# Other start addresses for the operands of the large matrix products

## The chip, the cores and the metric

The kernel runs on one core of a Trainium2 chip. The metric is the device time of one execution in microseconds (us); the time given is the median of several executions. The core has five engines with a queue each: TensorE (PE in the profile; its weight loads are listed apart as PEld), VectorE (DVE), ScalarE (ACT), GpSimd (POOL) and SyncE (SP), which here issues the DMAs. TensorE multiplies a stationary operand (up to 128 x 128, loaded by a weight load) with a moving operand (128 partitions, up to 512 columns), both read from the on-chip memory SBUF, and adds into PSUM. SBUF has 128 partitions; an address below is a byte offset within a partition, the same in all of them.

## The reference

A recurrent attention, then two mixing blocks, all in float32 (cut to what is computed):

```python
for t in range(S):                       # B=2, H=8, S=768, D=48
    cur = einsum('bhd,bhe->bhde', u * kt, vt)
    y[:, :, t] = einsum('bhd,bhde->bhe', rt, state + cur)
    state = wt[..., None] * state + einsum('bhd,bhe->bhde', kt, vt)
x = y as (B, S, 384)
h = gelu(x @ w_in)                       # 384 -> 1024, halves u and v
v_s = einsum('ts,bsd->btd', w_sg, norm(v) * g_ln) + b_sg
x = x + (u * v_s) @ w_out                # 512 -> 384
h = relu(xT @ w_tok1) @ w_tok2           # along the tokens, 768 -> 256 -> 768
u = x + hT
out = u + relu(u @ w_ch1) @ w_ch2        # 384 -> 1536 -> 384
```

## The kernel before, in words

The 1536 tokens (two batches of 768) are cut into 12 chunks of 128. Every product that isn't small is done three times: an operand is split into a high part, rounded to a 4-byte format that TensorE takes at one column per cycle (float32r in the listing), and a low part, the rest. `prod` (lines 254 to 259) issues high x high, high x low and low x high into one PSUM tile, so lines 257, 258 and 259 hold 588 matmuls each, 1764 in all. 1440 of them have 384 moving columns, 216 have 256 (`Hu`) and 108 have 512 (`Hv`); the stationary operand is always 128 x 128, and each matmul brings its own weight load.

The order is written out by hand. `ORDER` interleaves the attention of all chunks (letters for scores, states, outputs) with the input product `Hv` and `Hu`, the gate product `Gk` and the output product `Op`; `LAST` goes on with the rest of these, the token products `T1p` and `T2p` and the first quarter of the channel product `C1`; `rest` (line 483) then alternates one tile of `C1` for a quarter of the tokens with the three matmul groups of `C2` that use the quarter before. Each engine runs its instructions in that order. Weights arrive as pairs of 32-bit words in staging tiles `st`, are put together by ScalarE and VectorE (lines 214 to 219) and split into high and low (lines 224 to 226). SyncE issues all DMAs.

What matters here is where tiles lie. A pool reserves its buffers one after the other from the left end of SBUF, or from the right end with `side="right"`, when it is opened; a tile of a pool takes one of its buffers. The order of the pools and their sizes thus set every address before the program runs. The pools are: `dcst` (the identity matrix and small constants), `small` (statistics), `a2` (23 buffers of 2048 bytes: normalized gate operands `vh`, `vl`, token hidden `hh`, `hl`, channel hidden high `ch`), `a15` (36 of 1536: `x1h`, `uh`, `ul`, `gh`, `gl`, `cl` and others), `pw` and `psg` (six weights of 6144 each), `pst` (staging), later `pw2a` (`c10`, `c11`) on the left and `pxt` (the transposed input `xt`) on the right, where `pw2b` (`c12`) takes its place in the end. Since 2048, 1536, 6144 and 3072 are multiples of 512, all buffers of a pool have the same residue modulo 512, and slices of operands start at multiples of 512 bytes. `PAD` (line 37) gives three filler tiles, in 4-byte words, that nothing reads or writes.

Of the kernel before, what the change touches and what calls it, by code (L numbers as in the profile page):

```python
# [7 lines left out]
F32 = mybir.dt.float32  # L8
# [11 lines left out]
P = 128  # L20
# [13 lines left out]
ADDED = 7  # L34


PAD = 88, 32, 24


HALF = (slice(0, 64), slice(64, P))  # L40
# [33 lines left out]
class Dense:  # L74


    def __init__(self, tc, ctx, ins, out):
        self.tc, self.nc, self.ins, self.out = tc, tc.nc, ins, out
        self.ctx = ctx
        pool = lambda n, bufs, **kw: ctx.enter_context(  # L80
            tc.tile_pool(name=n, bufs=bufs, reuse_waits="tile", **kw))
        self.cst = pool("dcst", 1)
        self.cst.tile([P, PAD[0]], F32, name="pad0")
        self.ident = self.cst.tile([P, P], F32, name="ident")
        self.small = pool("small", 3, side="right")
        self.small.tile([P, PAD[2]], F32, name="pad2", bufs=1)
        self.pa2 = pool("a2", 23)
        self.pa15 = pool("a15", 36)
        self.pw = pool("pw", 6)
        self.psg = pool("psg", 6)  # L90
        self.pst = pool("pst", 4)
        self.ps3 = pool("mm3", 3, space=PSUM)
        self.banks = [self.ps3]
        self.x, self.v, self.vh, self.vl, self.uT = {}, {}, {}, {}, {}
        self.w, self.xt, self.xc, self.mv = {}, {}, {}, {}
        self.sums = None
        self.x1, self.u, self.gT, self.hid = {}, {}, {}, {}
        self.gps, self.gt, self.ops, self.tps, self.tok, self.ups = ({} for _ in range(6))
        self.todo, self.loaded, self.pipe = [], [], []

        self.free = [(self.pst, "st", 99)] * 4 + [(self.pw, "w", 2)] * 2
        self.n = 0
# [40 lines left out]
    def consts(self):  # L143
        nc = self.nc
        make_identity(nc, self.ident)
        self.g = self.cst.tile([P, FF // P], F32, name=self.nm("g"))
        self.mhalf = self.cst.tile([P, 1], F32, name=self.nm("mhalf"))
        nc.gpsimd.memset(self.mhalf, -0.5)
        warm = self.cst.tile([P, 1], F32, name=self.nm("warm"))
        nc.scalar.activation(warm, self.mhalf, AF.Gelu_apprx_tanh)  # L150
        self.cst.tile([P, PAD[1]], F32, name="pad1")

# [758 lines left out]
```

## Time and profile before

| | us |
|---|---|
| median of three runs | 390.88 (390.84 to 391.51) |
| the profiled execution | 391.98 |
| its span, first to last instruction | 390.3 |
| TensorE busy | 379.9 (97%) |
| VectorE busy | 233.5 (60%) |
| ScalarE busy | 187.8 (48%) |
| GpSimd busy | 133.1 (34%) |
| chain that ended last, TensorE's share | 83% |

The profiled execution is one of its own, so sums made from its rows are compared with its own 391.98 us first. In a timeline each row begins with the start and the length of an instruction in us; the length of a matmul includes the time its last column needs to come out, while the next one is already running, so the rate is read from start to start and not from the length. The chain follows the last instruction back to what released it, step by step.

### The profile page before, as it was taken

The page shows a single profiled execution, that of the slowest core. Times are in us where ns is not written, and L with a number is a line of the kernel's source. Part 1 is how long each engine was busy: PE and PEld are TensorE (multiplying, and loading weights), DVE is VectorE, ACT ScalarE, POOL GpSimd, SP SyncE. Part 2 cuts the span into 40 slices and gives each one's busy share as a digit, 9 for nine tenths or more (in the row PEclk, how much of TensorE's full clock was granted, in tenths as well). Part 3 has the DMA queues.
Part 4 walks back from the last instruction along what each step waited for, and adds up shares of the span by engine and source line. Part 5 has one row for each costly group of instructions (what it writes and reads, how often), then busy time and mean ns, then how long its engine had stood idle before and what let it go on. Part 6 is the DMA issues. An engine that isn't in the chain of part 4 may idle for free.

```text
span 390.3 us, 7950 instructions
## 1 busy us (share of the span) xinstructions
PE 379.9 (97%) x3229; PEld 354.8 (91%) x3229; DVE 233.5 (60%) x396; ACT 187.8 (48%) x427; POOL 133.1 (34%) x149
## 2 busy tenths in 40 slices
PE   8899999999999999999999999999999999999994
PEld 3487788889999799999999999999999999999993
DVE  7999998889797575794486674782133114211320
ACT  3699878887345795754546674741111111111000
POOL 2325577763543356567544651350000000000000
PEclk9999999999999999999999999999999999999998
DMA  7575375453361014322433242400010001000110
GB/s 238 172 215 181 100 246 155 122 156 114 94 214 42 2 40 123 107 66 71 123 102 102 81 126 78 121 3 0 3 44 18 1 0 62 0 2 0 64 40 27
DMA packets 15581, 33.68 MB, mean 86 GB/s; under 512 B 2352, under 2 KB 5680, under 8 KB 15536
## 3 DMA queue, kind: packets, MB, share of 16 engines
q1 hardware_dynamic: 15536, 33.09, 27.9%
q8 instruction: 27, 0.44, 0.5%
q14 instruction: 18, 0.15, 0.1%
HBM read 30.72 MB, written 2.36 MB: 85 GB/s over the span
## 4 chain that ended last, share of the span: by engine, by line
PE 83%; POOL 4%; ACT 3%; issue 3%; DVE 3%; DMA 2%; SPq 1%; POOLq 0%; ACTq 0%
PE mm L257 23%; PE mm L258 23%; PE mm L259 23%; PE py L623 3%; PE pa L582 2%; PE py L608 2%; DMA st<-in_dram 1%; PE tr L282 1%; POOL vs L367 1%; PE pkv L641 1%; DMA kr<-in_dram 1%; PE mm L567 1%; PE mm L420 1%; PE py L617 1%; PE pt L595 1%
## 5 line engine op out<-in xcount | busy, mean ns | idle before, releaser
L399 DVE SCALAR_TENSOR_TENSOR cl<-mm,ch 128x384 fp32r<-128x384 f32 x48 | 26.5, 556 | 83.9 <-ACT ch L398 83.9
L398 ACT ACTIVATE ch<-mm 128x384 fp32r<-128x384 f32 x48 | 23.4, 492 | 93.1 <-PE mm L259 93.0
L217 DVE SCALAR_TENSOR_TENSOR st<-st 128x384 int32<-128x384 int32 (+1 forms) x50 | 30.3, 607 | 9.5 <-ACT st L215 7.9
L219 DVE SCALAR_TENSOR_TENSOR st<-st 128x384 int32<-128x384 int32 (+1 forms) x50 | 33.2, 665 | 1.7
L214 ACT ACTIVATE st<-st 128x384 f32<-128x384 f32 (+1 forms) x50 | 25.8, 517 | 9.3 <-DMA st<-in_dram 9.3
L588 POOL TENSOR_SCALAR_AFFINE_SELECT A<-A 128x512 f32<-128x512 f32 x24 | 18.3, 770 | 33.5 <-ACT A L587 32.0
L215 ACT ACTIVATE st<-st 128x384 int32<-128x384 uint32 (+1 forms) x50 | 25.5, 510 | 0.0
L369 ACT ACTIVATE gh<-vs 128x384 fp32r<-128x384 f32 x16 | 8.4, 524 | 32.9 <-POOL vs L367 32.9
L367 POOL TENSOR_TENSOR vs<-vs,uT 128x384 f32<-128x384 f32 x16 | 19.2, 1205 | 11.6 <-DVE vs L365 11.6
L560 POOL TENSOR_TENSOR rk<-kr 112x512 f32<-112x512 f32 x12 | 19.0, 1580 | 11.4 <-DMA kr<-in_dram 11.4
L257 PE MATMUL mm<-xt,wuh 128*128 128x256 f32 x72 | 20.8, 289 | 0.0
L259 PE MATMUL mm<-xt,wul 128*128 128x256 f32 x72 | 20.3, 282 | 0.0
L258 PE MATMUL mm<-xt,wuh 128*128 128x256 f32 x72 | 20.3, 282 | 0.0
L534 DVE TENSOR_TENSOR_SCAN wf<-wf,scan 112x516 f32<-112x516 f32 x12 | 19.0, 1583 | 1.6 <-DMA wf<-in_dram 1.6
L548 DVE TENSOR_TENSOR_SCAN wf<-wf,scan 112x516 f32<-112x516 f32 x12 | 17.8, 1480 | 0.4
L391 POOL TENSOR_TENSOR x1l<-x,x1h 128x384 fp32r<-128x384 f32 x12 | 14.0, 1173 | 10.4 <-ACT x1h L390 10.4
L125 PE MATMUL mm<-scan 112*128 112x512 bf16 x49 | 14.2, 431 | 3.1 <-DVE scan L673 1.7
L556 DVE TENSOR_TENSOR kr<-kr,wf 112x1024 f32<-112x1024 f32 x12 | 15.9, 1328 | 1.2 <-DVE wf L548 0.2
L257 PE MATMUL mm<-ch,c20h 128*128 128x384 f32 x48 | 16.1, 336 | 0.2 <-DVE o L454 0.2
L257 PE MATMUL mm<-woh,gh 128*128 128x384 f32 x48 | 16.2, 338 | 0.0
L259 PE MATMUL mm<-woh,gl 128*128 128x384 f32 x48 | 16.1, 336 | 0.0
L257 PE MATMUL mm<-uh,c10h 128*128 128x384 f32 x48 | 16.1, 336 | 0.0
(188 smaller groups left out, 1233.3 us busy)
## 6 DMA issues: line engine op xcount, KB each, us to landing
st<-in_dram SPq DMA_DIRECT2D x38, 384.0 KB, 3.4
kr<-in_dram SPq DMA_DIRECT2D x12, 448.0 KB, 4.3
st<-in_dram SPq DMA_DIRECT2D x18, 256.0 KB, 4.2
wf<-in_dram SPq DMA_DIRECT2D x12, 227.5 KB, 2.9
vn<-in_dram SPq DMA_DIRECT2D x12, 192.0 KB, 4.5
out_dram<-o SPq DMA_DIRECT2D x12, 192.0 KB, 1.9
bsg<-in_dram SPq DMA_DIRECT2D x2, 192.0 KB, 3.9
ub<-in_dram SPq DMA_DIRECT2D x1, 3.5 KB, 4.6
```

The lines of the kernel that those rows point to most:

```text
L214: nc.scalar.activation(high.bitcast(F32), high.bitcast(F32), AF.Copy, scale=REBIAS)
L215: nc.scalar.activation(low, low.bitcast(U32), AF.Copy, scale=TOP3, bias=FLOOR)
L217: nc.vector.scalar_tensor_tensor(low, high, -2 ** 31, low, op0=ALU.bitwise_and, op1=ALU.bitwise_or)
L219: nc.vector.scalar_tensor_tensor(low, high, 3, low, op0=ALU.logical_shift_left, op1=ALU.bitwise_or)
L257: mm(out, w[0], x[0], start=first, stop=False, skip_group_check=True)
L258: mm(out, w[0], x[1], start=False, stop=False, skip_group_check=True)
L259: mm(out, w[1], x[0], start=False, stop=last, skip_group_check=True)
L367: nc.gpsimd.tensor_tensor(t, t, self.uT[d, h], op=ALU.mult)
L398: nc.scalar.activation(hi, ps, AF.Relu)
L399: nc.vector.scalar_tensor_tensor(lo, ps, 0.0, hi.bitcast(F32), op0=ALU.max, op1=ALU.subtract)
L534: nc.vector.tensor_tensor_scan(WF[i][:, WCOL + 2:], WF[i][:, :NHP * CW], scan1.rearrange("p h c -> p (h c)"), 0.0, op0=ALU.mult, op1=ALU.add)
L560: nc.gpsimd.tensor_tensor(RK[i][:PR], KR[i][:, 0], KR[i][:, 1], op=ALU.mult)
```

## The change

The pools are opened in another order, and the fillers are other ones. `dcst` moves from the left end to between `a15` and `pw`; `small` moves from the right end to the left, after `pst`; fillers may now stand in four places (a size of 0 opens none), and two of them are used, of 24 words (96 bytes) each.

```diff
-PAD = 88, 32, 24
+PAD = 24, 0, 0, 24
...
-        self.cst = pool("dcst", 1)
-        self.cst.tile([P, PAD[0]], F32, name="pad0")
-        self.ident = self.cst.tile([P, P], F32, name="ident")
-        self.small = pool("small", 3, side="right")
-        self.small.tile([P, PAD[2]], F32, name="pad2", bufs=1)
+        if PAD[0]:
+            pool("pada", 1).tile([P, PAD[0]], F32, name="pad0")
         self.pa2 = pool("a2", 23)
         self.pa15 = pool("a15", 36)
+        self.cst = pool("dcst", 1)
+        self.ident = self.cst.tile([P, P], F32, name="ident")
+        if PAD[1]:
+            pool("padb", 1).tile([P, PAD[1]], F32, name="pad1")
         self.pw = pool("pw", 6)
         self.psg = pool("psg", 6)
         self.pst = pool("pst", 4)
+        self.small = pool("small", 3)
+        if PAD[2]:
+            pool("padc", 1).tile([P, PAD[2]], F32, name="pad2")
+        if PAD[3]:
+            pool("padd", 1, side="right").tile([P, PAD[3]], F32, name="pad3")
...
-        self.cst.tile([P, PAD[1]], F32, name="pad1")
```

The start residues modulo 512, in bytes, as the two built programs have them:

| pool | before | after |
|---|---|---|
| `a2`, `a15`, identity | 0 | 256 |
| `pw`, `psg`, `pst` | 0 | 128 |
| `pw2a` (`c10`, `c11`) | 0 | 0 |
| `pxt` (`xt`), `pw2b` (`c12`) | 0 | 384 |

And the distance of the moving from the stationary operand, modulo 512, for the 1764 matmuls of lines 257 to 259:

| product | matmuls, columns | before | after |
|---|---|---|---|
| `Hv`, `Hu` (`xt` and `wv`, `wu`) | 108 of 512, 216 of 256 | 0 | 256 |
| `Gk` (`vh`, `vl` and `sg`) | 288 of 384 | 0 | 384 |
| `Op` (`gh`, `gl` and `wo`) | 144 of 384 | 0 | 384 |
| `T1p` (`x1h`, `x1l` and `t1`) | 72 of 384 | 0 | 128 |
| `T2p` (`hh`, `hl` and `t2`) | 72 of 384 | 0 | 384 |
| `C1` with `c10`, `c11` | 288 of 384 | 0 | 256 |
| `C1` with `c12` | 144 of 384 | 0 | 384 |
| `C2` (`ch`, `cl` and `c2`) | 432 of 384 | 0 | 128 |

The instructions of the executed path, their order on each engine, their shapes and what they wait for stay as they are.

## Rows read from the trace of the kernel before

**Rows 1.** The page: TensorE and the others, granted clock, the chain by engine.
```profile
PE 379.9 (97%) x3229; PEld 354.8 (91%) x3229; DVE 233.5 (60%) x396; ACT 187.8 (48%) x427; POOL 133.1 (34%) x149
...
PEclk9999999999999999999999999999999999999998
...
PE 83%; POOL 4%; ACT 3%; issue 3%; DVE 3%; DMA 2%; SPq 1%; POOLq 0%; ACTq 0%
```

**Rows 2.** Busy us per stretch: PE, PEld, DVE, ACT, POOL, then clock, DMA.
```profile
50.00:100.00 50.00, 50.00 (x645) 44.69 (x644) 45.57 (x70) 39.18 (x87) 32.65 (x34) 1.00 0.52 155
...
300.00:350.00 50.00, 50.00 (x291) 50.00 (x290) 11.71 (x22) 7.88 (x16) 0.00 (x0) 1.00 0.04 13
```

**Rows 3.** Timeline of TensorE, 299.9 to 302.9 us: start, length, instruction.
```profile
299.90 0.33 PE L257 MATMUL mm<-uh,c10h 128*128 128x384 f32 x1
...
300.42 0.33 PE L257 MATMUL mm<-uh,c11h 128*128 128x384 f32 x1
...
302.85 0.33 PE L259 MATMUL mm<-ch,c20l 128*128 128x384 f32 x1
```

**Rows 4.** Timeline of the weight loads in the same stretch.
```profile
300.42 0.19 PEld L258 LDWEIGHTS mm<-ul,c11h 128*128 128x128 f32 x1
```

**Rows 5.** Timeline of TensorE, two runs of 512 columns (ends of each).
```profile
44.11 0.39 PE L259 MATMUL mm<-wvh,xt 128*128 128x512 f32 x1
...
45.47 0.39 PE L259 MATMUL mm<-wvh,xt 128*128 128x512 f32 x1
...
134.33 0.40 PE L258 MATMUL mm<-wvl,xt 128*128 128x512 f32 x1
...
136.19 0.28 PE L257 MATMUL mm<-xt,wuh 128*128 128x256 f32 x1
```

**Rows 6.** Timeline of TensorE, a run of 256 columns (its ends).
```profile
150.05 0.28 PE L257 MATMUL mm<-xt,wuh 128*128 128x256 f32 x1
...
151.25 0.28 PE L258 MATMUL mm<-xt,wuh 128*128 128x256 f32 x1
```

**Rows 7.** Timeline of TensorE, warm-up in bf16, merged rows of two windows.
```profile
6.13 2.97 PE L125 MATMUL mm<-scan 112*128 112x512 bf16 x13
...
8.51 0.59 PE L125 MATMUL mm<-scan 112*128 112x512 bf16 x2
```

**Rows 8.** Timeline of TensorE, second token product near 246 us.
```profile
245.87 0.27 PE L420 MATMUL mm<-ident,x 128*128 128x128 f32 x1
...
246.16 0.34 PE L258 MATMUL mm<-t2l,hh 128*128 128x384 f32 x1
...
246.88 0.34 PE L259 MATMUL mm<-t2h,hl 128*128 128x384 f32 x1
```

**Rows 9.** Timeline of TensorE, three transposes, merged.
```profile
203.55 0.49 PE L420 MATMUL mm<-ident,x 128*128 128x128 f32 x3
```

**Rows 10.** Line 257 by stretch: matmuls, weight loads, clock, DMA.
```profile
45.90:130.70 84.80, 33.43 (x101) 19.08 (x101) 1.00 0.46 141
...
134.00:171.30 37.30, 24.78 (x76) 14.37 (x77) 1.00 0.29 85
171.30:201.70 30.40, 19.13 (x57) 10.66 (x57) 1.00 0.28 79
201.70:364.00 162.30, 102.46 (x304) 57.08 (x304) 1.00 0.14 42
...
365.70:391.00 25.30, 12.11 (x36) 6.76 (x36) 0.95 0.14 50
```

**Rows 11.** The chain that ended last, in order of time: start, length, what.
```profile
130.71 0.57 DVE x L632
...
180.03 0.81 POOL x1l L391
...
200.63 1.04 POOL t2l L226
...
384.77 0.56 DVE o L454
```

## Prediction

> **What bounds the kernel now.** The page comes first, [rows 1]: TensorE is busy 97% of the span, the clock line reads 9 in all slices but the last, and the chain that ended last is 83% TensorE. A busy TensorE isn't a TensorE at its peak, so the next view is the busy time by stretch, [rows 2]: from 50 to 100 us VectorE is busy for 45.57 of 50 us, close behind TensorE; from 300 to 350 us VectorE has 11.71 of 50 and TensorE all 50. The second half is therefore TensorE's alone; the first has two engines near the limit. The granted clock is 1.00 in these stretches, the upper of the two levels, 2.4 GHz.
>
> The third view is the order in time within a quiet stretch, [rows 3]. From 299.90 to 302.85 us there are 17 matmuls of 384 columns, one after the other: 2.95 / 17 = 173.5 ns from start to start. 384 columns at 2.4 GHz are 160.0 ns. So 13.5 ns of each matmul, 8% of it, is not columns, and no wait is named for it. Beside each matmul runs the weight load of the next one; it starts with the matmul [rows 3, 4], so the moving operand and the next stationary operand are read at the same time, from the first column on.
>
> Then I ask on what the 13.5 ns depends. With 512 columns a run of six takes 45.47 - 44.11 = 1.36 us, 226.7 ns each, against 213.3 of columns: 13.4 ns [rows 5]. With 256 columns ten take 151.25 - 150.05 = 1.20 us, 120.0 each, against 106.7: 13.3 ns [rows 6]. The excess is a fixed time, that of 32 columns (13.3 ns). A 128-column weight tile of 4-byte words is 512 bytes in a partition, and 32 columns are 128 bytes of it. The bf16 matmuls of the warm-up, which move half the bytes per column, don't have it: 13 in a row take 2.97 us and the last 2 of them 0.59, so 11 spacings take 2.38 us, 216.4 ns, 3.1 over the columns [rows 7]. They too read both operands from one place (the same tile), so a common address alone is no harm at half the byte rate.
>
> Is the excess a constant price? The trace says no. Another run with 512 columns takes 136.19 - 134.33 = 1.86 us for 8, 232.5 ns each, with the same shapes, lines and address residues as the run at 226.7 [rows 5]. And after the transposes of the second token product four 384-column matmuls take 246.88 - 246.16 = 0.72 us, 180 ns each [rows 8]. What differs there is only how the two read streams stand to each other in time after an interruption. A price that moves with that looks like two streams that get in each other's way, and an address shift is another way to move them apart.
>
> **The change part by part.** It adds, removes and reorders no executed instruction: pads and pool order set addresses alone. That part costs nothing, and there is no new wait and no transfer that is issued at another place. Vector, scalar and GpSimd instructions and the DMAs get other addresses too; the trace shows no price by address for them, their nearest evidence is that their operands also start at residue 0 now, and I put them at 0 with a bound of 0.5 us either way (about what a run of this kernel varies by: 390.84 to 391.51).
>
> What is left is the excess of the 1764 products with 4-byte operands. My reading: the weight load and the moving operand start at the same residue, the moving stream has to let the load go ahead by 128 bytes, and that is the 32 columns. When they start 128, 256 or 384 bytes apart and advance alike, they never meet, and the excess falls to what bf16 shows. To be careful with rounding I take 2.7 ns for that (between 2.38/11 = 216.4 and 216.0, less 213.3). The gain is then 13.5 - 2.7 = 10.8 ns per matmul. Bounds: 0 if the excess isn't an address matter, and at most 13.5 (no excess left). Downwards, the price of streams that don't fall into step, 180 - 173.5 = 6.5 ns lost per matmul.
>
> Could the weight load become the limit instead? Three transposes with a 128-column weight load each take 0.49 us, one alone 0.27, so two spacings take 0.22: 110 ns per load [rows 8, 9]. The products aim at 162.7, 109.4 and 216 ns; only those of 256 columns touch that limit, and they lose nothing that I count.
>
> How many of the 1764 lie where TensorE sets the pace? By the windows of line 257 [rows 10], times three (lines 258 and 259 have the same counts within one):
> 45.9 to 130.7 us: 101 x 3 = 303, 3.3 us. VectorE is 91% busy there [rows 2] and will be what is late next; I count half, 1.6.
> 134 to 171.3: 76 x 3 = 228, 2.5 us, counted in full.
> 171.3 to 201.7: 57 x 3 = 171, 1.8 us. The chain runs through GpSimd here [rows 11], from 180.03 to the low half of a weight at 200.63; how much of that GpSimd chain itself hangs on TensorE the chain doesn't settle. Half, 0.9.
> 201.7 to 364: 304 x 3 = 912, 9.8 us, in full: ScalarE and VectorE only follow there.
> 365.7 to 391: 36 x 3 = 108, 1.2 us, in full.
> Before 45.9 us and between 130.7 and 134 the chain is on other engines (from 130.71 VectorE's addition and what follows it, [rows 11]); nothing is counted. The end after 384.77 us (last addition, store) stays.
> Sum: 1.6 + 2.5 + 0.9 + 9.8 + 1.2 = 16.0 us. The profiled execution took 391.98 us, its span 390.3 and 1.7 around it; it would be 376.0. It was 1.1 over the median of 390.88, so the median becomes 374.9: 375. If all 1764 counted, 1764 x 10.8 ns = 19.1 us, 372. With half the gain per matmul the sum is 8.0 us, 383.
>
> The Trainium skill, "TensorE: Matmul & The Clock Gate", section "Back-to-back issue gap", gives N/2.4 + 2.5 ns for an isolated gap, 162.5 at 384 columns, which the trace contradicts by 11 ns in each matmul of rows 3; by that figure the sum would be 16.3 us (an estimate from the page). The same skill speaks against the change: "SBUF — State Buffer", section "Who interferes with whom", holds that TensorE's two read ports are independent and that "PE and ACT never wait on anyone", so addresses could not matter and the time would stay. The trace neither shows nor excludes that for two streams of one engine; the unequal runs of rows 5 lean against it.
>
> **The rivals.**
> No change, 390.9. The 32 columns could be a fixed step of loading 4-byte weights, whatever the address. For: the same 13.3 to 13.5 ns at three widths, undisturbed by the other engines [rows 2, 3, 5, 6], and at distance 0 alone the trace can't show a dependence on distance. Against: 232.5 and 180 ns [rows 5, 8]. The change then does only what it says, and the addresses do nothing. Chance 0.20.
>
> Part of the excess, 384. If only some of the distances are free (the products lie at 128, 256 and 384, and the load that runs beside a product's last matmul belongs to the next), or the load merely crosses the moving stream later, a third to two thirds goes: 5 to 11 us. Chance 0.18.
>
> Slower, 400. At distance 0 the streams fall into a steady step: 173.5 ns holds for hundreds of matmuls, and disturbed runs come back to it. That may be the best they can do: the load first, the moving stream one block behind, no further meeting. With unequal starts the step may never form, and each matmul pays what the disturbed ones do. The place is every 384-column product, 1440 of them; the price 180 - 173.5 = 6.5 ns, 9.4 us in all, and nothing hides it since TensorE is the bound: 400. It decides as soon as the mean spacing in the channel stage is above 173.5. For: the disturbed runs of rows 5 and 8 are slower than the steady ones. Against: they are disturbed by interruptions, with the same residues. Chance 0.20.
>
> **How the numbers follow.** Full removal 0.42 at 375 (own range 371 to 381), part of it 0.18 at 384, nothing 0.20 at 390.9, slower 0.20 at 400. Faster is 0.60. What can be told from no change is about 0.2%, 0.8 us: same 0.20, slower 0.20. Cases of both signs hold the chance, so the range is wide: below 372 I leave 0.05, and above 396, where the upper half of the slower case lies, about 0.12.
>
> **What would show it.** Right: from 300 us on the spacing of 384-column matmuls at 162 to 164 ns, about 110 with 256 columns and 216 with 512; TensorE waiting more in 46 to 131 us on VectorE and ScalarE, and near 200 us on GpSimd; the channel stage from 202 us to the end about 11 us shorter. Wrong: 173.5 again (the fixed price); three different spacings by pool (C1 from the first late pool at 256, its last third at 384, C2 at 128), which is the partial case and says which distance is good; or 175 and more (the slower case).

## The result and the profile after

The changed kernel is slower: 393.62 us (392.84 to 394.80, six executions) against 390.99 us (390.83 to 392.40, six) in the same comparison, ratio 1.0062 with a 95% interval of 1.0047 to 1.0078. The medians differ by 2.63 us, the interval means 1.8 to 3.0 us lost, where 16 us of gain had been forecast. The profiled execution took 392.84 us.

The page of the kernel after, busy time, granted clock and chain by engine (to be held against [rows 1]; all line numbers are 5 higher than before):

```profile
PE 382.2 (98%) x3229; PEld 357.6 (91%) x3229; DVE 232.7 (59%) x396; ACT 188.1 (48%) x427; POOL 132.6 (34%) x149
...
PEclk9999999999999999999999999999999999999998
...
PE 93%; ACT 4%; DVE 1%; issue 0%; ACTq 0%
```

The same 3229 matmuls at the same granted clock keep TensorE busy 2.3 us longer, while the other engines move by less than 1 us. TensorE's share of the chain rose from 83% to 93%, so nothing else became the bound; the products themselves got slower.

Where, the order in time shows. Timeline of TensorE after, the channel stage (start, length, instruction), one round of 18 products, to be held against [rows 3]:

```profile
299.84 0.33 PE L262 MATMUL mm<-uh,c10h 128*128 128x384 f32 x1
...
301.41 0.34 PE L262 MATMUL mm<-ch,c20h 128*128 128x384 f32 x1
...
302.99 0.33 PE L262 MATMUL mm<-uh,c10h 128*128 128x384 f32 x1
```

The first nine, `C1` (six with `c10` and `c11` at 256, three with `c12` at 384), take 301.41 - 299.84 = 1.57 us, 174.4 ns each; the nine of `C2`, whose operands are 128 bytes apart, take 1.58 us, 175.6 each; the round 3.15 us, 175.0 on average, where [rows 3] gave 173.5. Not one product came near the 162 to 164 ns of the forecast.

The gate product has one distance, 384, over a long stretch. Timeline of TensorE after, gate stage:

```profile
162.82 0.34 PE L262 MATMUL mm<-sg0h,vh 128*128 128x384 f32 x1
163.00 0.34 PE L263 MATMUL mm<-sg0l,vh 128*128 128x384 f32 x1
163.17 0.34 PE L264 MATMUL mm<-sg0h,vl 128*128 128x384 f32 x1
...
166.34 0.34 PE L264 MATMUL mm<-sg0h,vl 128*128 128x384 f32 x1
```

From 162.82 to 166.34 us are 20 spacings: 3.52 / 20 = 176.0 ns. In the records, which have whole nanoseconds, five spacings repeat: 173, 174, 175, 182, 176. At a distance of 0 they are 173 and 174 alone. So the streams do settle, but into a longer pattern.

For the whole stage, two rows of each kernel: the first matmul of the twelfth tile of `C1`, and the last product. Timeline of TensorE before, then after:

```profile
251.19 0.33 PE L257 MATMUL mm<-uh,c10h 128*128 128x384 f32 x1
...
384.40 0.34 PE L259 MATMUL mm<-ch,c22l 128*128 128x384 f32 x1
```

```profile
250.65 0.34 PE L262 MATMUL mm<-uh,c10h 128*128 128x384 f32 x1
...
385.28 0.34 PE L264 MATMUL mm<-ch,c22l 128*128 128x384 f32 x1
```

Between them 133.21 us became 134.63, 1.42 us of the loss. The rest lies earlier, in the gate, output and token products. Grouping all spacings between a product's matmul and the next one, from the records of both profiled executions, gives the mean in ns:

| product (matmuls) | distance after | before | after | (after - before) x count, us |
|---|---|---|---|---|
| `C2` (431) | 128 | 174.56 | 176.98 | 1.04 |
| `C1` with `c10`, `c11` (288) | 256 | 173.64 | 174.00 | 0.10 |
| `C1` with `c12` (144) | 384 | 173.64 | 176.47 | 0.41 |
| `Gk` (288) | 384 | 174.63 | 176.88 | 0.65 |
| `Op` (144) | 384 | 175.42 | 177.26 | 0.26 |
| `T1p` (72) | 128 | 173.33 | 176.01 | 0.19 |
| `Hu` (216) | 256 | 122.56 | 122.75 | 0.04 |
| `Hv` (108) | 256 | 244.37 | 244.37 | 0.00 |

The sum is 2.69 us, the difference of the medians 2.63; that they come out so near is partly luck, since the interval allows 1.8 to 3.0. The two profiled executions themselves differ by 0.86 us only (391.98 and 392.84): the one after is 1.16 us ahead from the 18th microsecond on (see the last section), and its 72 matmuls of `T2p` take 190.82 ns on average against 200.17, 0.67 us less; 2.69 - 1.16 - 0.67 = 0.86. (The before column of `C1` is the mean of all its matmuls; `T2p` is left out of the table, since its means hold waits and transposes.) Products at 256 lose next to nothing; those at 128 and 384 lose about 2.4 ns each.

### The profile page after: what moved, and what is told of

The parts are those of the page before. It is cut to its first block, busy times and chain, and to the rows that moved or that the text cites. A ratio compares the mean times of both kernels' runs of the same rounds, so it can differ in the third digit from the quotient of the medians.

```text
span 391.1 us, 7950 instructions
## 1 busy us (share of the span) xinstructions
PE 382.2 (98%) x3229; PEld 357.6 (91%) x3229; DVE 232.7 (59%) x396; ACT 188.1 (48%) x427; POOL 132.6 (34%) x149
## 4 chain that ended last, share of the span: by engine, by line
PE 93%; ACT 4%; DVE 1%; issue 0%; ACTq 0%
PE mm L262 26%; PE mm L264 25%; PE mm L263 25%; PE py L628 3%; PE pa L587 3%; PE mm L131 2%; PE py L613 2%; PE mm L572 1%; PE pkv L646 1%; PE tr L287 1%; PE py L622 1%; PE mm L425 1%; PE pt L600 1%; ACT wf L669 1%; ACT st L219 0%
## 5 line engine op out<-in xcount | busy, mean ns | idle before, releaser
L539 DVE TENSOR_TENSOR_SCAN wf<-wf,scan 112x516 f32<-112x516 f32 x12 | 17.8, 1481 | 1.6 <-DMA wf<-in_dram 1.5
L553 DVE TENSOR_TENSOR_SCAN wf<-wf,scan 112x516 f32<-112x516 f32 x12 | 17.7, 1478 | 0.4
L264 PE MATMUL mm<-uh,c12l 128*128 128x384 f32 x48 | 16.4, 341 | 0.0
L263 PE MATMUL mm<-wol,gh 128*128 128x384 f32 x48 | 16.2, 338 | 0.0
L263 PE MATMUL mm<-cl,c22h 128*128 128x384 f32 x48 | 16.2, 338 | 0.0
## 6 DMA issues: line engine op xcount, KB each, us to landing
wf<-in_dram SPq DMA_DIRECT2D x12, 227.5 KB, 2.9
```

The lines of the kernel that those rows point to most:

```text
L263: mm(out, w[0], x[1], start=False, stop=False, skip_group_check=True)
L264: mm(out, w[1], x[0], start=False, stop=last, skip_group_check=True)
```

## The experiments

Three of the kernels are the kernel before with blocks of matmuls added after its last product (`probe`), which use one weight tile of `c20` as moving operand and one tile of `u` as stationary one; their results are not used, and their times are not compared with the kernel's. Each ran once, at a granted clock of 1.00. In these the spacing is the distance of two rows' starts, divided by the matmuls between them (32 in a row, 0.3 ns per hundredth of a us).

### 1. The price against the distance, measured by itself

```diff
+        W, U = self.w["c20"][0], self.u[3, 0][0]
+        for _ in range(32): mm(ps[:128, :384], U[:, 0:128], W[:, 0:384], start=True, stop=True)  # s0
+        for _ in range(32): mm(ps[:128, :384], U[:, 32:160], W[:, 0:384], start=True, stop=True)  # s128
+        for _ in range(32): mm(ps[:128, :384], U[:, 0:128], W[:, 32:416], start=True, stop=True)  # m128
...
```

> The kernel before with 40 blocks of 32 matmuls each after its last product; their results go nowhere, the output is that of the kernel before. A block takes one stationary slice (128 columns of a uh tile) and one moving slice (384 columns of a c20 weight, 4-byte operands) again and again; from block to block the start of the stationary slice is shifted by 0 to 480 bytes, or that of the moving one, or both; further blocks have 256 or 512 moving columns, 64 or 32 stationary columns, or bf16. Read from each: the time from start to start. Theory H (half the modulus): the distance counts modulo 256; 0 and 256 give 173.3 ns, 128 and 384 an unsteady mean near 176, whichever operand is shifted, and both shifted by 128 give 173.3 again. Rival D (any distance): 256 is unlike 0 too, 175 or more. Rival A (absolute starts): what counts is that an operand starts off a multiple of 256; both shifted by 128 are then as slow as one. On the excess over the columns: if it is the time of the load's own reading, 64 stationary columns give half of it, 16 columns' time, 166.7 ns at 384, and 32 columns 163.3; if it is a fixed price, 173.3 stays. My prediction, that some distance frees the excess, needs a block near 162.5.

Timeline of TensorE, the kernel with the first blocks (a row is 32 matmuls merged; L464 distance 0, L468 stationary operand 128 further, L476 384, L488 both 128 further, L494 and L495 512 columns at 0 and 128, L500 a stationary operand of 32 columns, L501 and L502 bf16 at 0 and 128):

```profile
389.21 5.71 PE L464 MATMUL mm<-c20h,uh 128*128 128x384 f32 x32
394.75 5.71 PE L465 MATMUL mm<-c20h,uh 128*128 128x384 f32 x32
...
411.45 5.80 PE L468 MATMUL mm<-c20h,uh 128*128 128x384 f32 x32
417.08 5.81 PE L469 MATMUL mm<-c20h,uh 128*128 128x384 f32 x32
...
456.19 5.80 PE L476 MATMUL mm<-c20h,uh 128*128 128x384 f32 x32
461.83 5.81 PE L477 MATMUL mm<-c20h,uh 128*128 128x384 f32 x32
...
523.28 5.71 PE L488 MATMUL mm<-c20h,uh 128*128 128x384 f32 x32
528.83 5.74 PE L489 MATMUL mm<-c20h,uh 128*128 128x384 f32 x32
...
549.63 7.45 PE L494 MATMUL mm<-c20h,uh 128*128 128x512 f32 x32
556.91 7.61 PE L495 MATMUL mm<-c20h,uh 128*128 128x512 f32 x32
564.36 7.42 PE L496 MATMUL mm<-c20h,uh 128*128 128x512 f32 x32
...
590.28 5.71 PE L500 MATMUL mm<-c20h,uh 128*32 128x384 f32 x32
595.83 7.08 PE L501 MATMUL mm<-c20h,uh 128*128 128x512 bf16 x32
602.75 7.07 PE L502 MATMUL mm<-c20h,uh 128*128 128x512 bf16 x32
```

Read row to row: at 0, (394.75 - 389.21) / 32 = 173.1 ns; at 128, 5.63 / 32 = 175.9; at 384, 5.64 / 32 = 176.3. With both operands moved by 128 it is 173.4 again: the distance counts, not the place. The settled spacing in the records (the mean of a block's last twenty spacings before its final one), for the stationary operand moved by so many bytes:

| moved by | ns | moved by | ns |
|---|---|---|---|
| 0, 256 | 173.35, 173.3 | 128, 384 | 176.0, 176.0 |
| 32, 288 | 173.3, 173.35 | 160, 416 | 176.65, 176.7 |
| 64, 320 | 174.65, 174.7 | 192, 448 | 173.35, 173.3 |
| 96, 352 | 173.35, 173.35 | 224, 480 | 176.65, 176.7 |

Two things follow. The pattern repeats after 256 bytes, so the change's four distances were in truth two, 0 and 128. And no distance goes below 173.3. Nor does a shorter load lower it: 32 stationary columns, a quarter of the load, leave (595.83 - 590.28) / 32 = 173.4. With 64 stationary columns the two distances change places, 176.65 settled at 0 and 173.35 at 128, so the table holds for loads of 128 columns. In bf16 it is 6.92 / 32 = 216.3 for 512 columns, the same as [rows 7], and 128 bytes change nothing there. At 512 columns a distance of 0 gives 7.28 / 32 = 227.5 and 128 gives 232.8.

### 2. The pools' order alone, all distances 0

```diff
-PAD = 24, 0, 0, 24
+PAD = 24, 32, 32, 56
```

(against the kernel after)

> The kernel after, its pool order kept, with the fillers set to 24, 32, 32, 56 words: all operands of the large products start at residue 256, their distance is 0. Theory H and D (the distance makes the difference): the time of the kernel before, 391.0 us, ratio 1.000 within 0.002. Rival O (the order of the pools and other engines' addresses do it): as the kernel after, 1.006. Rival A (absolute starts off 0 modulo 512 cost): 1.006 as well.

390.85 us against 390.71 of the kernel before, ratio 1.0003 [0.9991, 1.0015]. The new order of pools, with all large operands at residue 256, costs nothing; nor do the new addresses of everything else.

### 3. 1620 of the products at 256

```diff
-PAD = 24, 0, 0, 24
+PAD = 24, 96, 32, 56
```

> The kernel after with the fillers 24, 96, 32, 56: 1620 of the 1764 products have a distance of 256, the 144 with c12 a distance of 0; none is at 128 or 384. Theory H: 391.0 us, ratio 1.000 within 0.002. Rival D: every product is off 0 but 144, so at least the loss of the kernel after, 1.006 to 1.009.

390.77 us, ratio 1.0006 [0.9992, 1.0021]. Timeline of TensorE of this kernel, one round of the channel stage:

```profile
299.92 0.33 PE L262 MATMUL mm<-ch,c20h 128*128 128x384 f32 x1
...
303.04 0.33 PE L262 MATMUL mm<-ch,c21h 128*128 128x384 f32 x1
```

18 spacings in 3.12 us are 173.3 ns: 256 is as good as 0.

### 4. 1440 of the products at 128 or 384

```diff
-PAD = 24, 0, 0, 24
+PAD = 24, 0, 32, 24
```

> The kernel after with the fillers 24, 0, 32, 24: the 288 products of C1 with c10 and c11 move from distance 256 to 128, so 1440 instead of 1152 products are at 128 or 384. Theory H with 2.6 ns for each product that isn't in step: 1440 x 2.6 = 3.7 us if all stay out of step, 394.7 us, ratio 1.0096; since C1 at 256 brings the streams back into step in the kernel after, more than in proportion to the counts (1.0062 x 1440/1152 would be 1.0078). Rival O: as the kernel after, 1.006.

394.18 us, ratio 1.0076 [1.0055, 1.0098]. Timeline of TensorE of this kernel, the same round:

```profile
299.81 0.34 PE L262 MATMUL mm<-ch,c20h 128*128 128x384 f32 x1
...
302.97 0.34 PE L262 MATMUL mm<-ch,c20h 128*128 128x384 f32 x1
```

18 spacings in 3.16 us are 175.6 ns. Now `C1` with `c10` and `c11` lies at 128 as well, and its mean is 176.08 where it was 174.00 at 256 in the kernel after. So the loss goes where the distance goes. It is the spacing that shows this: the ratios of this kernel and of the kernel after are too close for their intervals to tell them apart.

### 5. Which pair of streams, and where the 32 columns come from

```diff
+        for _ in range(16): mm(ps[:128, :384], U[:, 0:128], W[:, 0:384], start=True, stop=True); mm(ps[:128, :384], U[:, 32:160], W[:, 32:416], start=True, stop=True)  # alt_own0
+        for _ in range(16): mm(ps[:128, :384], U[:, 0:128], W[:, 32:416], start=True, stop=True); mm(ps[:128, :384], U[:, 32:160], W[:, 0:384], start=True, stop=True)  # alt_own128
+        for _ in range(16): mm(ps[:128, :384], U[:, 0:128], W[:, 0:384], start=True, stop=True); mm(p2[:128, :384], U[:, 0:128], W[:, 0:384], start=True, stop=True)  # alt_bank
+        for _ in range(32): mm(ps[:128, :128], U[:, 0:128], W[:, 0:128], start=True, stop=True)  # n128
...
```

In the first block each matmul's own operands are 0 apart, while the weights that are loaded beside it are 128 away from its moving operand; in the second it is the other way round. Behind the alternations come other widths, distances and numbers of stationary columns.

> The kernel before with 29 further blocks of 32 matmuls after its last product, results unused, the output that of the kernel before. Two blocks alternate between two matmuls: in the first, both operands of one matmul start at 0 and both of the next at 128, so a matmul's own operands are 0 apart and a moving operand and the weights loaded beside it (those of the next matmul) are 128 apart; in the second it is the reverse. Theory L (the weight load meets the moving operand that runs beside it): the first near 176 ns, the second 173.3. Rival W (own operands): the reverse. A sweep of moving columns at distance 0 (128 to 480): theory F (a fixed price of 32 columns): columns + 32 at 2.4 GHz, 66.7 ns at 128, 133.3 at 288, 153.3 at 336, 200 at 448. Rival G (a grid: the spacing goes to the next whole 32 columns above the columns): 336 and 368 give 160.0 or 173.3 instead of 153.3 and 166.7. Rival P (a share of the columns, 8%): 57.8 ns at 128. With 512 columns and the moving operand 64 on: 226.7 if the step holds as at 384 (173.3), else up to 233; with 256 columns and the weights at 64 it was 117.8, at 96, 160 and 224 between 117 and 120. 16 and 96 stationary columns at 173.3 if the price doesn't depend on the load's length.

Timeline of TensorE, the kernel with the second blocks (L463 own operands at 0, L464 own at 128, L465 two PSUM tiles in turn, all 384 columns; L466 the next block):

```profile
389.51 5.77 PE L463 MATMUL mm<-c20h,uh 128*128 128x384 f32 x32
395.12 5.82 PE L464 MATMUL mm<-c20h,uh 128*128 128x384 f32 x32
400.77 5.71 PE L465 MATMUL mm<-c20h,uh 128*128 128x384 f32 x32
406.32 3.68 PE L466 MATMUL mm<-c20h,uh 128*128 128x128 f32 x32
```

Own operands at 0: 5.61 / 32 = 175.3 ns; own at 128: 5.65 / 32 = 176.6; two PSUM tiles: 173.4. Both orders are slower than 173.3, so neither the product's own distance alone nor that to the load beside it alone sets the price, and both plain theories fall in part. The widths, settled spacings from the records: 288 columns take 131.65 ns, 320 146.65, 352 160.0, 368 166.65, 400 180.0, 416 188.3, 448 202.7, 480 216.7. From 320 to 400 that is the time of the columns plus 32 (13.3 ns) with no steps; at 416 to 480 it is up to 16.7 ns over the columns, at 288 only 11.7. 128, 192 and 224 columns all take 111.7: about the floor of 110 ns of the weight load that the prediction read off [rows 8, 9]. 16 and 96 stationary columns at 384 moving ones settle at 175.0 and 173.35, and 64 at 173.2, where experiment 1 had 176.65. With 512 moving columns four more distances (stationary 32, 96 and 160 further, moving 64 further) settle between 228.75 and 234.15, against 226.65 at 0, although 32 and 96 cost nothing at 384.

### 6. Hu at -64, Hv and the last third of C1 at +64

```diff
-PAD = 88, 32, 24
+PAD = 88, 32, 40
```

(against the kernel before)

> The kernel before with its third filler at 40 instead of 24 words: xt and c12 move down by 64 bytes. Hu (216 of 256 columns) is then at moving minus stationary of -64, Hv (108 of 512) and C1 with c12 (144 of 384) at +64, all else at 0. By the first probe Hu gains 120.0 - 117.8 = 2.2 ns each, at most 0.5 us, half of it behind VectorE; c12 stays at 173.3. Theory H with the sign: ratio 0.999 to 1.000, not to be told from 1. Rival (only multiples of 256 are in step): 252 products lose 1.3 to 6 ns, 1.001 to 1.002.

391.21 us against 390.79, ratio 1.0017 [1.0005, 1.0028]. Timeline of TensorE of this kernel, a run of `Hu`, then the channel stage:

```profile
146.40 0.28 PE L257 MATMUL mm<-xt,wuh 128*128 128x256 f32 x1
...
149.68 0.28 PE L259 MATMUL mm<-xt,wul 128*128 128x256 f32 x1
...
299.78 0.34 PE L259 MATMUL mm<-uh,c12l 128*128 128x384 f32 x1
299.96 0.35 PE L257 MATMUL mm<-ch,c20h 128*128 128x384 f32 x1
...
301.54 0.33 PE L257 MATMUL mm<-uh,c10h 128*128 128x384 f32 x1
```

`Hu` gains: 3.28 us for 29 spacings, 113.1 ns against 120.0 in [rows 6]. But `C2`, left at distance 0, loses: the nine from 299.96 take 1.58 us, 175.6 each, and its mean over the kernel is 176.33 against 174.56. It follows the `c12` products, which are now 64 bytes apart; the first three spacings behind them here are 185, 176 and 181 ns in the records. Something costs that belongs to no single distance: the change from one to the next.

### 7. Distances of +96 and -96

```diff
-PAD = 24, 0, 0, 24
+PAD = 24, 56, 8, 32
```

(against the kernel after; 504 products at +96, 648 at -96, 612 at 0)

> The kernel after with the fillers 24, 56, 8, 32: moving minus stationary is +96 for 504 products (Gk, Op, T2), -96 for 648 (C2, T1, C1 with c12) and 0 for the rest; none is at 128. Theory H with the sign, from the first probe (+96 is its shift of 160 modulo 256, 176.65 ns; -96 its shift of 96, 173.35): 504 x 3.3 ns = 1.7 us, 392.4 us, ratio 1.0043, and in the trace the gate and output products near 176.6 and C2 at 173.4. Rival (128 alone is bad): 1.000. Rival (sign plays no part): both groups slow, 1152 x 3.3 = 3.8 us, 1.0097.

393.27 us, ratio 1.0070 [1.0057, 1.0084], more than the distances by themselves would make it. `Gk` (177.46) and `Op` (177.88), at +96, are slow as in the first blocks (176.7 for a moving operand 96 ahead, listed there as a stationary one moved by 416), and `C2` at -96 (174.76) is near its 173.4 there. The excess is in the first two thirds of `C1`, which are at 0: mean 177.70. Timeline of TensorE of this kernel, where they begin:

```profile
300.50 0.35 PE L262 MATMUL mm<-uh,c10h 128*128 128x384 f32 x1
...
301.05 0.33 PE L262 MATMUL mm<-uh,c11h 128*128 128x384 f32 x1
```

Between them lie three spacings, 0.55 / 3 = 183 ns each, right after the change from -96 to 0.

### 8. The change of distance by itself

```diff
+        for st, mv in (((0, 0),) * 9 + ((64, 0),) * 9) * 3: mm(ps[:, :384], U[:, st:st + 128], W[:, mv:mv + 384], start=True, stop=True)  # mix_0_256
+        for st, mv in (((0, 0),) * 9 + ((0, 16),) * 9) * 3: mm(ps[:, :384], U[:, st:st + 128], W[:, mv:mv + 384], start=True, stop=True)  # mix_0_m64
+        for st, mv in (((0, 0),) * 9 + ((8, 0),) * 9) * 3: mm(ps[:, :384], U[:, st:st + 128], W[:, mv:mv + 384], start=True, stop=True)  # mix_0_s32
+        for st, mv in (((0, 0),) * 9 + ((32, 0),) * 9) * 3: mm(ps[:, :384], U[:, st:st + 128], W[:, mv:mv + 384], start=True, stop=True)  # mix_0_s128
+        for st, mv in (((0, 0),) * 9 + ((16, 16),) * 9) * 3: mm(ps[:, :384], U[:, st:st + 128], W[:, mv:mv + 384], start=True, stop=True)  # mix_0_both64
...
```

> The kernel before with further blocks after its last product, results unused, the output that of the kernel before. Five blocks change between 9 matmuls at distance 0 and 9 at another, three times over (54 in all, 384 columns): the other is 256; +64 and -32, which keep 173.3 ns when they stand alone; 128, which doesn't; and both operands moved by 64. Theory C (a change of distance throws the streams out of step for some matmuls, and each distance has its own step): 256 and both by 64 stay at 173.4, +64 and -32 rise to 174 to 176 although neither costs alone, 128 to 175 or more. Rival (each matmul pays for its own distance alone): +64 and -32 stay at 173.4, 128 gives the mean of 173.3 and 176.0, 174.7. Then 384 columns with the weights at 16, 48, 80 to 240 bytes: none below 173.3 if the 32 columns are a floor; one near 162.5 would bring back my prediction. Then 256 columns with the weights at 16 to 240 bytes: the kernel's own Hu took 113 to 114 ns at -64 in the run before, so some below 117.

Timeline of TensorE, the kernel with the third blocks (a row of L463 to L467 is 54 matmuls, nine at 0 and nine at: 256; moving 64 further; stationary 32 further; stationary 128 further; both 64 further):

```profile
388.54 9.52 PE L463 MATMUL mm<-c20h,uh 128*128 128x384 f32 x54
397.90 9.56 PE L464 MATMUL mm<-c20h,uh 128*128 128x384 f32 x54
407.30 9.60 PE L465 MATMUL mm<-c20h,uh 128*128 128x384 f32 x54
416.74 9.62 PE L466 MATMUL mm<-c20h,uh 128*128 128x384 f32 x54
426.20 9.66 PE L467 MATMUL mm<-c20h,uh 128*128 128x384 f32 x54
435.70 5.81 PE L468 MATMUL mm<-c20h,uh 128*128 128x384 f32 x32
```

In that order 9.36, 9.40, 9.44, 9.46 and 9.50 us: 173.3, 174.1, 174.8, 175.2 and 175.9 ns each. 0 and 256 mix freely. A moving operand 64 further and a stationary one 32 further cost nothing when they stay (both settled at 173.3 in experiment 1) but do when they alternate with 0; in the records about six or seven spacings after a change are off. The last row missed its expectation of 173.4: both operands moved by 64 keep a distance of 0 between own operands and still cost most. At the seam the moving operand of one place runs beside the load of the other, as in the first block of experiment 5; that this is the reason wasn't tested by itself. Eight distances from 16 to 240 in steps of 32, six of them new, settled between 173.3 and 177.35; none was lower. With 256 columns a stationary operand 64 further settles at 113.35 ns, the fourteen other distances from 16 to 240 between 116.65 and 123.3, against 120.0 at 0 and 256 in experiment 1. In experiment 1 the same block (64 further) took 117.8, and at 384 columns a stationary operand 16 further took 173.35 there and 176.65 here. So a distance alone doesn't fix the pattern; what ran before is the difference between these blocks, and what in it decides wasn't isolated.

### 9 and 10. Hu at -64, all 384-column products at 0

Experiment 6 lost in `C2` what it won in `Hu`. A filler of 448 bytes ahead of `pw2b` takes `c12` back to 0.

```diff
-PAD = 88, 32, 24
+PAD = 88, 32, 40
...
+        pool("pade", 1).tile([P, 112], F32, name="pad4")
```

> The kernel before with its third filler at 40 words, and one more filler of 112 words at the right end ahead of the last weight pool: Hu at -64 and Hv at +64 as in the run with 40 words alone, but c12 back at 0, so all products after them are at 0. Theory C: the channel products keep 173.4 ns, Hu gains about 3.8 ns each (118.8 against 122.6 mean), 0.8 us at most, part of it behind VectorE: ratio 0.998 to 0.9995. Rival (the loss of that run came from elsewhere): 1.0017 again.

389.85 us against 391.56, ratio 0.9962 [0.9948, 0.9976]. The same code again, for a second interval:

> The kernel with Hu at -64, Hv at +64 and all else at 0 once more, since its trace accounts for 0.4 us and its ratio said 1.5. Theory C, by the trace: ratio 0.9985 to 0.9995 (0.2 to 0.6 us). Rival (its gain is real and partly elsewhere): 0.996 to 0.997 again.

389.87 us against 390.77, ratio 0.9975 [0.9963, 0.9987]. It is faster than the kernel before, by 0.25 to 0.4%. Timeline of TensorE, the first of the two (experiment 9), a run of `Hu`:

```profile
147.03 0.28 PE L258 MATMUL mm<-xt,wuh 128*128 128x256 f32 x1
...
150.99 0.28 PE L260 MATMUL mm<-xt,wul 128*128 128x256 f32 x1
```

35 spacings in 3.96 us, 113.1 ns. The mean of all `Hu` matmuls is 118.82 against 122.56, which over 216 is 0.81 us; `C2` and `C1` are back at 174.56 and 173.64, as before. The medians differ by 1.71 and 0.90 us, and the first is more than the trace accounts for. The medians of the new code agree (389.85 and 389.87 us); it is the kernel before that took 391.56 us in the first comparison, 0.6 to 0.9 us more than in every other one here (390.71 to 390.99). So the second ratio is the better measure; why the kernel before was slower that once wasn't settled.

### 11. The kernel before again

The code is that of the kernel before, with no edit.

> The kernel before, unchanged, as a control in the same rounds. Ratio 1.000 within its interval; if it is off by 0.003 in either direction, a part of the previous ratio was the start of the executions and not the addresses.

390.83 us against 390.77, ratio 0.9998 [0.9988, 1.0008]: no difference shows where there is none. So 0.9975, from the same comparison, is a difference, and 1.0062 is far outside such an interval too.

## Why the prediction was wrong

**The bound.** TensorE was named as what sets the pace, and that held: the spacings of its products sum to 2.69 us, within the 1.8 to 3.0 that were lost. No other engine took over, so the halves counted for VectorE and GpSimd don't matter to the outcome.

**No price for the other operands' addresses and the order of pools.** Put at 0 with 0.5 us either way. Experiment 2 gives +0.14 us, with an interval of -0.4 to +0.6.

**The failing step: "When they start 128, 256 or 384 bytes apart and advance alike, they never meet, and the excess falls to what bf16 shows."** At 384 columns, where most of the sum lies, it doesn't fall at all: the settled spacing of loads of 128 columns is 173.3 ns or more at all 26 distances tried, so the 13.3 ns aren't the moving stream that waits for a load at the same residue. They also remain when the load is a quarter as long (173.4). The gain of 10.8 ns per matmul and the whole sum of 16.0 us go with that step. What the 13.3 ns are stays open: they are there with 4-byte operands and loads of 16 to 128 columns, and not in bf16. Nor are they the fixed time of 32 columns that the prediction read from three widths: at distance 0 the excess is 11.7 ns at 288 columns and up to 16.7 at 416 to 480, and with 256 columns a distance of -64 takes the spacing from 120.0 to 113.1, 6.9 of the 13.3 ns. But the change put `Hu` and `Hv` at 256, where experiment 1 gives 120.0 and 226.65 ns, the same as at 0.

**How it came to fail.** The step rested on the question whether the excess is a constant price, which was answered with the runs at 232.5 and 180 ns [rows 5, 8]. Those were dearer than the steady ones. They show that something can be added to the price, not that the price can be taken away; a cheaper run would have been needed for that, and the trace had none at 384 columns. Experiment 1 has such an extra at a distance (232.8 ns at 512 columns) and, for a few matmuls, at none: its block of 512 columns at distance 0 begins with spacings of 233, 236, 229, 232 and 231 ns before it settles at 226.65. Experiment 8 shows the like behind a mere change of operands. Whether the 180 ns behind the transposes come from that too wasn't shown.

**The 110 ns of a weight load as a limit.** Experiment 5 gives 111.7 ns for 128 to 224 columns. That bound was right and had no use here.

**The rivals.** "Slower" came nearest: at a distance of 128 or 384 the steady step of 173.3 doesn't form, a longer pattern takes its place, and it shows in the mean spacing of the channel stage. But unequal starts as such aren't the cause, since 256, or a stationary operand 32 or 96 bytes further, keep 173.3, and its picture of a moving stream one block behind the load wasn't tested. Its size was off. 6.5 ns on 1440 products was read from four matmuls behind transposes, that is from the dearest spacings of a disturbance; what counts is the mean of the repeating pattern, 2.4 ns, and the 288 of `C1` at 256 pay nothing: 1152 x 2.4 ns = 2.8 us, not 9.4. "No change" was right about the 13.3 ns at 384 columns, wrong that addresses do nothing. "Part of the excess" falls: its sign, three spacings by pool, did appear (174.0 at 256, 176.5 at 384, 177.0 at 128), but all of them above the old one.

The page "SBUF — State Buffer" of the Trainium skill, section "Who interferes with whom", has TensorE's moving operand and weight load read through independent ports and says that PE never waits on anyone. By that the time would have stayed. In experiment 1 only the distance of these two operands differs, and the spacing goes from 173.35 to 176.0 ns; the measurement decides: where the two operands lie to each other does change the pace, by a little. Which part of the chip makes it so isn't shown.

## What to carry to other kernels

An irregular run that is slower than the steady one is no evidence that the steady price can be lowered: before operands are padded, measure a block of equal products at several distances by itself, which here settled the question in one run. With loads of 128 columns, keep the distance of the two operands of such 4-byte products at 0 modulo 256, which was free at 384 and 512 columns, and the same from product to product, since a change costs even where each distance alone is free. With 256 columns -64 was better, by 0.25% of the kernel's time. Pools may change their order as long as these residues stay.

## What the runs showed of the hardware

The repeat after 256 bytes, the sign of the distance (+96 costs 3.3 ns, -96 nothing) and the change's own cost are told above. One more thing disturbs the comparison of single executions. Near 12.3 us an elementwise product on GpSimd and a scan on VectorE meet, and whichever starts first makes the other long. Timeline of both engines before, then after:

```profile
12.29 1.28 POOL L560 TENSOR_TENSOR rk<-kr 112x512 f32<-112x512 f32 x1 [5.77 <-DMA kr<-in_dram]
12.36 2.30 DVE L534 TENSOR_TENSOR_SCAN wf<-wf,scan 112x516 f32<-112x516 f32 x1
```

```profile
12.26 1.22 DVE L539 TENSOR_TENSOR_SCAN wf<-wf,scan 112x516 f32<-112x516 f32 x1
12.48 2.08 POOL L565 TENSOR_TENSOR rk<-kr 112x512 f32<-112x512 f32 x1 [6.06 <-DMA kr<-in_dram]
```

The scan takes 2.30 us behind the product and 1.22 ahead of it; the product 1.28 or 2.08. The same page of the Trainium skill ("SBUF — State Buffer", section "Who interferes with whom") says that an instruction of VectorE with two SBUF inputs and one of GpSimd that reads SBUF exclude each other, with which this agrees. The start decides it by 0.07 to 0.22 us. At the 18th microsecond the profiled execution after is thus 1.16 us ahead of that before, and experiment 11, the same code as before, is 1.0 us ahead. So two single profiled executions (392.84 and 391.98 us) differ by less than the medians do, and a term of a few us is compared by spacings and medians, not by two spans.
